# Retention in 64-token chunks for the first twelve rows too: 64x64 products, two of a row's four product lists one burst late

## The chip, the cores and the metric

The kernel runs on one core of a Trainium2 chip. Its metric is the device time of one execution in microseconds (us), lower is better. PE is the matrix engine TensorE, PEld its loading of weights, DVE is VectorE, ACT is ScalarE, POOL is GpSimd, and SP is the engine whose queue issues most DMAs. PSUM holds the sums of PE in eight banks of 512 f32 columns.

## The reference

Multi-head retention, and a feed-forward layer on its output. Shapes: 4 sequences, 8 heads, 768 tokens, 64 dimensions per head; the layer goes from 512 to 2048 and back, on 3072 tokens.

```python
gamma = 1.0 - 2.0 ** (-5.0 - np.arange(H))
scale = 1.0 / np.sqrt(D)
for t in range(S):
    state = gamma[None, :, None, None] * state + np.einsum('bhd,bhe->bhde', k[:, :, t], v[:, :, t])
    y[:, :, t] = scale * np.einsum('bhd,bhde->bhe', q[:, :, t], state)
x = y.transpose(0, 2, 1, 3).reshape(B * S, H * D)
h = x @ w_in
g = h * np.clip(h + 3.0, 0.0, 6.0) / 6.0
return g @ w_out
```

Over a piece of tokens the same y is the masked product of scores (q times k, only earlier tokens) with v, plus q times the state of the tokens before the piece, with the decay gamma laid on v and on y as powers.

## The kernel before, in words

**Rows.** The 3072 tokens are 24 rows of 128 tokens (six rows to a sequence), the eight heads are four pairs. `load(r)` fetches a row's four tiles: `kt` and `qt` (k and q with the dimension of a head pair on the 128 partitions), `vn` and `kn` (tokens on the partitions). The first eight rows (`AHEAD`) go into the large `early` tiles, with the odd rows' `kn` in buffers that later rows use (`SPARE`); the rows behind them use two buffers or one each (`BUFS`). Decays: rows 0 to 11 have them on v (`decay`: on ACT in eight instructions per row for rows 0 to 7, on GpSimd behind that) and on y (`load_decay` fetches the table `dq`); rows 12 to 23 have them on k and q (`scale`).

**Rows 0 to 11: `burst`.** PE's work for row r, and for the rest of row r-1, is one uninterrupted burst: products of the old row's q with its state (L268, eight, 64x64 weights, 128 columns); scores of the new row (L281, two per head, 64x64 weights, 128 and 64 columns) into `sc`, two PSUM banks; the old row's masked scores `am` with its v (L292, eight, 128x64 weights, 128 columns) into y; then DVE takes y times `dq` (L301) and `split` makes of it a high and a low part (ACT, DVE; L140, L141) as x. Last come the new row's sums of k times v (L314, eight, 128x64 weights) into `uz`, which ACT copies to SBUF as the state of row r+1 (L323), and DVE masks the new scores (L327: 1024 columns, all of `sc`). `am`, `sc` and `y` have one buffer each.

**Rows 12 to 23: `chunk_burst`.** A row is two chunks of 64 tokens, and all its products are 64x64 with 64 columns, in four lists of 16: `scores`, `sums` (into `uz`), `past` (q times state) and `inner` (masked scores times v). `together` sets two products of one list beside two of another. Half of `sc` and of `y` serves even rows and half odd rows; `keep(n)` is ACT's copy of `uz` as the state before chunk n. All its PE instructions are recorded as L349, its copies of `uz` as L353, and its mask product, 512 columns, as L392. `am` uses half of its tile; the other half is the buffer of the odd rows' `kn`.

**The layer.** `mm1(u, jj)` multiplies weight block jj with x of four rows (u): 12 matmuls of 128x512 into h (L464), three for each product of split numbers; ACT and DVE make g of it (L468, L469), which goes to memory. Three buffers of h. `build_w1` and `build_w2` make split f32 weights out of the 64-bit ones, on DVE and ACT (L122 to L141). Behind the last row (302 us) the output products run (L605).

**Order.** PE's order is written out by hand: bursts 0 to 4, then `mm1` for u = 0, with bursts 5 to 8 between its first four blocks; then blocks of u = 0 and u = 1 by turns, with bursts 8 to 12 (rows 8 to 11) among those of u = 1, then u = 2 and on with the chunked rows. Burst 8 is in two parts (old row, new row). `keep_busy` adds matmuls without use behind early bursts. The instructions of the other engines are ordered by a planner at compile time, by the order of the text and its own estimate of when each is ready; on the chip each engine keeps that order.

Of the kernel before, what the change touches and what calls it, by code (L numbers as in the profile page):

```python
# [28 lines left out]
def retention_ffn(ctx: ExitStack, tc: tile.TileContext, qkv, w_in, w_out, dvs, dqs, dkc, dqc, dmc, out, B, H, S, D):  # L29
# [37 lines left out]
    cst_sb = const.tile([P, ROWS_B, H], F32, name="cst_sb")  # L67
    nc.scalar.dma_start(out=cst_sb.rearrange("p n h -> p (n h)"), in_=dvs)
# [3 lines left out]
    mask = const.tile([P, 2, NPAIR // 2, P], F32, name="mask")  # L72
    nc.gpsimd.memset(mask, 1.0)
    for a in range(2):
        for b in range(2):
            m = mask[b * D : (b + 1) * D, a]
            nc.gpsimd.affine_select(
                out=m, in_=m, pattern=[[0, NPAIR // 2], [1, P]], compare_op=ALU.is_ge, fill=0.0, base=-D * (a ^ b), channel_multiplier=-1
            )
    ccst = const.tile([P, ROWS_B, 2 * NPAIR], F32, name="ccst")  # L80
# [112 lines left out]
    nc.vector.memset(sc, 0.0)  # L193
# [3 lines left out]
    def load(r):  # L197
# [7 lines left out]
        for i, (x, n) in enumerate((("kt", 1), ("qt", 0), ("vn", 3), ("kn", 2))):  # L205
            o = r % 2 * 4 + i
            if r < AHEAD and o < 7:
                t[x] = early[r // 2 * 2][:, o]
            elif x == "kn" and r > CHUNKED and r % 2:
                t[x] = both["am"][:, 1]  # L210
            else:
                tag = SPARE[r // 2] if r < AHEAD else f"l{x}"
                t[x] = apool.tile([P, NPAIR, P], F32, tag=tag, name=nm(x), bufs=BUFS[tag])
            m = NPAIR * P
            if x == "kn" and r % ROWS_B == ROWS_B - 1:
                m = m // 2 if r >= CHUNKED else 0
            if m:
                nc.sync.dma_start(out=t[x].rearrange("p h n -> p (h n)")[:, 0:m], in_=qkv[r, n][:, 0:m])
        if r >= CHUNKED:
            t["vn"], t["kn"] = (  # L220
                t[x].rearrange("p h n -> p (h n)").rearrange("p (c a e) -> p c a e", c=2, e=D) for x in ("vn", "kn")
            )
# [14 lines left out]
    def decay(r):  # L237
        v = rows[r]["vn"].rearrange("p a (h e) -> p (a h) e", h=2)
        if r < AHEAD:
            for h in range(H):  # L240
                nc.scalar.activation(  # L241
                    out=v[:, h], in_=v[:, h], func=AF.Copy, scale=cst_sb[:, r % ROWS_B, h : h + 1]
                )
        else:
            nc.gpsimd.tensor_tensor(
                out=v, in0=v, in1=cst_sb[:, r % ROWS_B, :, None].to_broadcast([P, H, D]), op=ALU.mult
# [12 lines left out]

    def burst(r, new=True, old=True):  # L260

        new, old = new and rows.get(r), old and rows.get(r - 1)
        if old:
            old["y"] = ps_a.tile([P, 2, NPAIR, P], F32, tag="y", name=nm("y"))
            if "state" in old:
                for p in range(NPAIR):
                    for h, pr in enumerate(halves):
                        nc.tensor.matmul(  # L268
                            place_y(old["y"], p, h),
                            old["state"][pr, p],  # L270
                            old["qt"][pr, p],
                            start=p < 2,
                            stop=False,
                            skip_group_check=True,
                        )
        if new:
            for p in range(NPAIR):
                for c in range(2):
                    for h, pr in enumerate(halves):
                        tokens = slice(0, P) if c == 0 else halves[1]  # L280
                        nc.tensor.matmul(  # L281
                            sc[halves[h ^ p % 2 ^ c], h, place_am(p, h), tokens],
                            new["kt"][pr, p, halves[c]],
                            new["qt"][pr, p, tokens],
                            start=True,
                            stop=True,
                            skip_group_check=True,
                        )
        if old:
            for p in range(NPAIR):  # L290
                for h in (p % 2, 1 - p % 2):
                    nc.tensor.matmul(  # L292
                        place_y(old["y"], p, h),
                        old["vn"][:, p, halves[h]],
                        old["am"][:, h, place_am(p, h)],
                        start=p < 2 and "state" not in old,
                        stop=True,
                        skip_group_check=True,
                    )
            x = apool.tile([P, NPAIR, P], F32, tag="xr", name=nm("xr"))  # L300
            nc.vector.tensor_tensor(  # L301
                out=x.rearrange("p (h a) n -> p h a n", h=2),
                in0=old["y"][:, :, 0 : NPAIR // 2],
                in1=old["dq"].rearrange("p (h a) n -> p h a n", h=2),
                op=ALU.mult,
            )
            split(*x_place(r - 1), x)
            del rows[r - 1]
        if new:
            n = r % ROWS_B  # L310
            if n < ROWS_B - 1:
                for p in range(NPAIR):
                    for pr in halves:
                        nc.tensor.matmul(  # L314
# [330 lines left out]
def chunked(rows):  # L645

    return rows // 2
# [87 lines left out]
```

## Time and profile before

| | |
|---|---|
| Time, three runs | 587.98, 589.79, 589.87 us; median 589.79 |
| Profiled execution | 588.39 us, span 586.7 us from the first to the last instruction |
| Granted PE clock, mean | 0.996 |
| First h (`mm1`) | starts at 30.3 us, and with more than one matmul at 31.8 |
| Bursts of rows 0 to 11 | 6 to 142 us |
| Chunked rows | 142 to 302.7 us |
| Output products | from 302.7 us on, L605 231.5 us of PE |

In the tables of groups, a line gives source line, engine, operation, output and inputs, shapes, count, busy time in all, mean ns of one, and idle time ahead of it with what ended it. In lists in order of time, the first number is the start in us, the second the time taken, and a bracket gives the idle time before and what released it. Matmuls are pipelined, and one's end is modelled, so the time of a run of them is taken from start to start.

### The profile page before, as it was taken

The page shows a single profiled execution, that of the slowest core. Times are in us where ns is not written, and L with a number is a line of the kernel's source. Part 1 is how long each engine was busy: PE and PEld are TensorE (multiplying, and loading weights), DVE is VectorE, ACT ScalarE, POOL GpSimd, SP SyncE. Part 2 cuts the span into 40 slices and gives each one's busy share as a digit, 9 for nine tenths or more (in the row PEclk, how much of TensorE's full clock was granted, in tenths as well). Part 3 has the DMA queues.
Part 4 walks back from the last instruction along what each step waited for, and adds up shares of the span by engine and source line. Part 5 has one row for each costly group of instructions (what it writes and reads, how often), then busy time and mean ns, then how long its engine had stood idle before and what let it go on. Part 6 is the DMA issues. An engine that isn't in the chain of part 4 may idle for free.

```text
span 586.7 us, 11328 instructions
## 1 busy us (share of the span) xinstructions
PE 571.7 (97%) x4604; PEld 469.8 (80%) x4604; DVE 416.2 (71%) x589; ACT 249.4 (43%) x393; POOL 36.5 (6%) x39
## 2 busy tenths in 40 slices
PE   8888999999999999999999999999999999999997
PEld 7776788787788888888888888888888888888885
DVE  4879999999533498333225989769786697866881
ACT  5674545444423344332324555434335344344430
POOL 1010000200211121122000000000000000000000
PEclk9989999999999999999999999999999999999999
DMA  8974777565865467565243557564844747635611
GB/s 319 391 280 162 238 246 258 205 228 199 278 207 191 168 226 256 179 184 175 92 131 121 180 206 242 171 223 142 271 161 144 226 142 276 218 95 193 214 73 72
DMA packets 59028, 117.05 MB, mean 200 GB/s; under 512 B 5984, under 2 KB 6624, under 8 KB 58976
## 3 DMA queue, kind: packets, MB, share of 16 engines
q1 hardware_dynamic: 44864, 91.01, 47.4%
q10 hardware_dynamic: 14112, 25.33, 11.4%
q8 instruction: 36, 0.59, 0.4%
q14 instruction: 16, 0.13, 0.1%
HBM read 84.85 MB, written 31.46 MB: 198 GB/s over the span
## 4 chain that ended last, share of the span: by engine, by line
PE 78%; DVE 14%; DMA 3%; issue 3%; ACT 1%; SPq 1%; ACTq 0%; DVEq 0%
PE o L605 39%; PE h L464 33%; DVE g L469 2%; DVE we L131 2%; PE uz L349 2%; DMA st<-in_w_in 2%; DVE wb L128 2%; DVE am L327 2%; PE sc L349 1%; DVE ww L134 1%; PE y L349 1%; DVE w L141 1%; DVE x L141 1%; DMA early<-in_qkv 1%; DVE xr L301 1%
## 5 line engine op out<-in xcount | busy, mean ns | idle before, releaser
L464 PE MATMUL h<-x,w 128*128 128x512 f32 x1152 | 271.1, 394 | 3.9 <-DVE g L469 1.8
L464 PEld LDWEIGHTS h<-x,w 128*128 128x128 f32 x1152 | 215.4, 189 | 52.2 <-DVE g L469 2.9
L605 PE MATMUL o<-gc,w 128*128 128x512 f32 x1008 | 231.5, 392 | 0.0
L605 PEld LDWEIGHTS o<-gc,w 128*128 128x128 f32 x1008 | 189.2, 188 | 42.1
L469 DVE SCALAR_TENSOR_TENSOR g<-g,h 128x512 f32<-128x512 f32 x96 | 65.3, 683 | 84.6 <-ACT g L468 84.6
L468 ACT ACTIVATE g<-h,three 128x512 f32<-128x512 f32 x96 | 65.3, 684 | 100.6 <-PE h L464 88.6
L140 ACT ACTIVATE gc<-gv 128x1024 fp32r<-128x1024 f32 x48 | 50.8, 1060 | 64.7 <-PE o L605 54.2
L141 DVE TENSOR_TENSOR gc<-gv,gc 128x1024 fp32r<-128x1024 f32 x48 | 58.6, 1221 | 23.8 <-ACT gc L140 23.8
L140 ACT ACTIVATE gc<-spare 128x1024 fp32r<-128x1024 f32 x36 | 38.2, 1061 | 50.3 <-PE o L605 39.9
L141 DVE TENSOR_TENSOR gc<-spare,gc 128x1024 fp32r<-128x1024 f32 x36 | 43.9, 1219 | 9.8 <-ACT gc L140 9.8
L140 ACT ACTIVATE w<-ww 128x384 fp32r<-128x384 f32 (+2 forms) x34 | 18.7, 555 | 48.6 <-DVE ww L134 46.1
L126 ACT ACTIVATE we<-we,ebias 128x512 int32<-128x512 int32 x32 | 22.9, 717 | 11.9 <-DVE we L122 11.9
L134 DVE SCALAR_TENSOR_TENSOR ww<-wb,we 128x512 f32<-128x512 f32 x32 | 25.3, 790 | 0.6
L235 POOL TENSOR_TENSOR qs<-qt,dq 128x512 f32<-128x512 f32 x12 | 16.8, 1397 | 96.7 <-PE y L349 74.1
L128 DVE SCALAR_TENSOR_TENSOR wb<-st,wb 128x512 f32<-128x512 uint32 x32 | 22.0, 686 | 0.3
L131 DVE SCALAR_TENSOR_TENSOR we<-st,we 128x512 int32<-128x512 int32 x32 | 22.1, 691 | 0.0
L141 DVE TENSOR_TENSOR w<-ww,w 128x384 fp32r<-128x384 f32 (+2 forms) x34 | 19.9, 590 | 3.1 <-ACT w L140 3.1
L96 DVE TENSOR_TENSOR spare<-gv 128x1024 f32<-128x1024 f32 x12 | 14.6, 1220 | 6.4 <-DMA gv<-gd 6.4
L122 DVE TENSOR_SCALAR we<-st 128x512 int32<-128x512 int32 x32 | 13.5, 421 | 7.7 <-DMA st<-in_w_in 7.4
L93 DVE TENSOR_TENSOR spare<-spare,gv 128x1024 f32<-128x1024 f32 x12 | 14.7, 1221 | 5.4 <-DMA gv<-gd 5.4
L241 ACT ACTIVATE early<-early,cst_sb 128x64 f32<-128x64 f32 x64 | 16.4, 336 | 4.3 <-DMA early<-in_qkv 4.3
L93 DVE TENSOR_TENSOR gv<-gv 128x1024 f32<-128x1024 f32 x12 | 14.7, 1223 | 4.8 <-DMA gv<-gd 4.5
(73 smaller groups left out, 392.7 us busy)
## 6 DMA issues: line engine op xcount, KB each, us to landing
gd<-g ACTq DMA_DIRECT2D x96, 256.0 KB, 2.6
gv<-gd SPq DMA_DIRECT2D x48, 512.0 KB, 4.9
gv<-gd SPq DMA_DIRECT2D x48, 256.0 KB, 3.1
st<-in_w_in SPq DMA_DIRECT2D x16, 512.0 KB, 4.1
st<-in_w_out SPq DMA_DIRECT2D x16, 512.0 KB, 3.7
early<-in_qkv SPq DMA_DIRECT2D x28, 256.0 KB, 6.0
kt<-in_qkv SPq DMA_DIRECT2D x16, 256.0 KB, 3.8
qt<-in_qkv SPq DMA_DIRECT2D x16, 256.0 KB, 4.6
```

Of the source, the lines that this page charges most:

```text
L93: return nc.vector.tensor_tensor(out=out_, in0=a, in1=b, op=ALU.subtract)
L126: nc.scalar.activation(out=e, in_=e, func=AF.Relu, scale=8.0, bias=ebias)
L128: nc.vector.scalar_tensor_tensor(out=y, in0=lo.bitcast(U32), scalar=2.0**-32, in1=b, op0=ALU.mult, op1=ALU.add)
L131: nc.vector.scalar_tensor_tensor(out=e, in0=hi, scalar=-2147483648, in1=e, op0=ALU.bitwise_and, op1=ALU.bitwise_or)
L134: nc.vector.scalar_tensor_tensor(out=w, in0=y, scalar=2.0**-20, in1=e.bitcast(F32), op0=ALU.mult, op1=ALU.mult)
L140: nc.scalar.activation(out=hi, in_=src, func=AF.Copy)
L141: nc.vector.tensor_tensor(out=lo, in0=src, in1=hi, op=ALU.subtract)
L349: nc.tensor.matmul(out_, lhs, rhs, start=start, stop=True, skip_group_check=True)
L464: nc.tensor.matmul(h, t[:, o, a], xs[u][b][:, k], start=k + n == 0, stop=(k, n) == (NK - 1, 2), skip_group_check=True)
L468: relu = nc.scalar.activation(out=g, in_=h, func=AF.Relu, bias=three)
L469: ins = nc.vector.scalar_tensor_tensor(out=g, in0=g, scalar=6.0, in1=h, op0=ALU.min, op1=ALU.mult)
L605: nc.tensor.matmul(acc[i][h] if last else acc[i][:, h], w2c[j][:, RIGHT[i], x, h], gc[:, y, jj], start=j == 0 and n == 0, stop=j == NFP - ...
```

## The change

Rows 0 to 11 take the products of the chunked rows, with their own decays. The layout of q, k, v is by chunk for all rows, and tables fall to match (`dvs` goes, `ccst` is loaded at the start in its place; its columns now scale v). The mask becomes 64x64 per head, repeated, and the mask product 512 columns wide (`weigh`, shared). `sc`, `y` and `am` are used by halves for all rows; `sc` is no longer cleared. `burst` issues, for the old row, the sums over chunk 0 beside the products with the state ahead of chunk 0, ACT's copy of `uz`, then the scores of the new row beside the old row's inner products, the mask product, then the old row's sums over chunk 1 beside the products with the state just copied, and another copy. So sums, states and inner products all belong to row r-1, scores to row r. The last row of a sequence loads the first half of its `kn`, which it did not need before.

```diff
-    cst_sb = const.tile([P, ROWS_B, H], F32, name="cst_sb")
-    nc.scalar.dma_start(out=cst_sb.rearrange("p n h -> p (n h)"), in_=dvs)
+    ccst = const.tile([P, ROWS_B, 2 * NPAIR], F32, name="ccst")
+    nc.scalar.dma_start(out=ccst.rearrange("p n h -> p (n h)"), in_=dkc)
...
-    mask = const.tile([P, 2, NPAIR // 2, P], F32, name="mask")
+    mask = const.tile([P, NPAIR, D], F32, name="mask")
...
-    nc.vector.memset(sc, 0.0)
...
-            elif x == "kn" and r > CHUNKED and r % 2:
+            elif x == "kn" and r > AHEAD and r % 2:
                 t[x] = both["am"][:, 1]
...
             if x == "kn" and r % ROWS_B == ROWS_B - 1:
-                m = m // 2 if r >= CHUNKED else 0
+                m = m // 2
...
+    def score(r):
+        new = rows[r]
+        s = chunks(sc, r)
+        new["am"] = chunks(both["am"], 0)
+        return [[(s[pr, c, p], new["kt"][pr, p, halves[c]], new["qt"][pr, p, halves[c]], True) for p, h, pr in sides] for c in range(2)]
+
+    def weigh(r, table):
+        nc.vector.tensor_tensor(
+            out=rows[r]["am"].rearrange("p c a t -> p c (a t)"),
+            in0=chunks(sc, r).rearrange("p c a t -> p c (a t)"),
+            in1=table[:, None, :].to_broadcast([P, 2, NPAIR * D]),
+            op=ALU.mult,
+        )
+
     def burst(r, new=True, old=True):
         new, old = new and rows.get(r), old and rows.get(r - 1)
+        scores = score(r) if new else [[], []]
+        sums, past, inner = ([[], []] for _ in range(3))
         if old:
+            y, n = both["y"][:, r % 2], (r - 1) % ROWS_B
+            for p, h, pr in sides:
+                for c in range(2):
+                    out_ = y[halves[1 - h], p, halves[c]]
+                    if c == 0 or n < ROWS_B - 1:
+                        sums[c].append((uz[pr, p], old["kn"][pr, c, p], old["vn"][pr, c, p], n + c + p == 0))
+                    if n + c:
+                        past[c].append((out_, ("state", c, pr, p), old["qt"][pr, p, halves[c]], c + p == 0))
+                    inner[c].append((out_, old["vn"][pr, c, p], old["am"][pr, c, p], n + c + p == 0))
+        together(sums[0], resolve(past[0], r - 1))
+        if sums[0]:
+            keep(2 * r - 1)
+        together(scores[0], inner[0])
+        together(scores[1], inner[1])
         if new:
+            weigh(r, mask.rearrange("p a n -> p (a n)"))
+        together(sums[1], resolve(past[1], r - 1))
+        if sums[1]:
+            keep(2 * r)
         if old:
             x = apool.tile([P, NPAIR, P], F32, tag="xr", name=nm("xr"))
+            nc.vector.tensor_tensor(out=x, in0=y, in1=old["dq"], op=ALU.mult)
             split(*x_place(r - 1), x)
             del rows[r - 1]
...
         decay(0)
+        both["am"] = apool.tile([P, 2, NPAIR, P], F32, tag="am", name=nm("am"), bufs=1)
+        both["y"] = ps_a.tile([P, 2, NPAIR, P], F32, tag="y", name=nm("y"))
...
             if r == AHEAD:
-                nc.sync.dma_start(out=ccst.rearrange("p n h -> p (n h)"), in_=dkc)
                 nc.sync.dma_start(out=cmask, in_=dmc)
```

All matmuls of the old `burst` fall away with this. `resolve` puts the state that is there by then in place of its name. `chunk_burst` takes its scores and mask product from `score` and `weigh`, with the work that it had.

More of the change, by code (lines that the diff above doesn't have):

```diff
@@ L263, in burst @@
         if old:
[L264 to L275, printed above, removed]
@@ L276, in burst @@
-        if new:
[L277 to L288, printed above, removed]
@@ L289, in burst @@
-        if old:
[L290 to L299, printed above, removed]
-            x = apool.tile([P, NPAIR, P], F32, tag="xr", name=nm("xr"))
[L301 to L306, printed above, removed]
+            y, n = both["y"][:, r % 2], (r - 1) % ROWS_B
@@ L307, in burst @@
             split(*x_place(r - 1), x)
             del rows[r - 1]
[L309 to L314, printed above, removed]
-                            uz[pr, p],
-                            new["kn"][:, p, pr],
-                            new["vn"][:, p, pr],
-                            start=n == 0 and p == 0,
-                            stop=True,
-                            skip_group_check=True,
-                        )
-                before[r + 1] = apool.tile([P, NPAIR, D], F32, tag="state", name=nm("state"), bufs=3)
-                nc.scalar.activation(out=before[r + 1], in_=uz, func=AF.Copy)
-            if r in before:
-                new["state"] = before.pop(r)
-            new["am"] = apool.tile([P, 2, NPAIR, P], F32, tag="am", name=nm("am"), bufs=1)
-            nc.vector.tensor_tensor(
-                out=new["am"].rearrange("p h a n -> p h (a n)"),
-                in0=sc.rearrange("p h a n -> p h (a n)"),
-                in1=mask.rearrange("p a b n -> p (a b n)")[:, None, :].to_broadcast([P, 2, NPAIR * P]),
-                op=ALU.mult,
-            )
@@ L334, in x_place, with resolve @@
+    def resolve(todo, r):
+        return [(out_, before[2 * r + lhs[1]][lhs[2], lhs[3]], rhs, start) for out_, lhs, rhs, start in todo]
     def x_place(r):
@@ L357, in chunk_burst @@
         new, old = rows.get(r), rows.get(r - 1) if r > CHUNKED else None
-        if r == CHUNKED:
-            both["y"] = ps_a.tile([P, 2, NPAIR, P], F32, tag="y", name=nm("y"))
-            both["am"] = apool.tile([P, 2, NPAIR, P], F32, tag="am", name=nm("am"), bufs=1)
-        sums, scores, past, inner = ([[], []] for _ in range(4))
-        sides = [(p, h, halves[h]) for p in range(NPAIR) for h in range(2)]
+        sums, past, inner = ([[], []] for _ in range(3))
+        scores = score(r) if new else [[], []]
         if new:
-            s = sc[:, r % 2].rearrange("p a n -> p (a n)").rearrange("p (c a n) -> p c a n", c=2, n=D)
-            new["am"] = both["am"][:, 0].rearrange("p a n -> p (a n)").rearrange("p (c a n) -> p c a n", c=2, n=D)
             for p, h, pr in sides:
-                for c in range(2):
-                    scores[c].append((s[pr, c, p], new["kt"][pr, p, halves[c]], new["qt"][pr, p, halves[c]], True))
                 first = r % ROWS_B == 0 and p == 0
@@ L391, in chunk_burst @@
         if new:
-            nc.vector.tensor_tensor(
-                out=new["am"].rearrange("p c a t -> p c (a t)"),
-                in0=s.rearrange("p c a t -> p c (a t)"),
-                in1=cmask[:, None, :].to_broadcast([P, 2, NPAIR * D]),
-                op=ALU.mult,
-            )
+            weigh(r, cmask)
         if old:
@@ L724 @@
         "in_w_out": lay_w_out(moe_w_out),
-        **{f"in_decays_{n}": a for n, a in zip("vykqs", constants(H, S, D))},
+        **{f"in_decays_{n}": a for n, a in zip("ykqs", constants(H, S, D))},
     }
```

60 lines of the change are left out of this document (21 added, 39 removed).

## The prediction

> **What bounds the kernel now.** I read the page's busy shares first, then busy times by stretch, then the chain that ended last in order of time, then the orders on TensorE (PE) and ScalarE (ACT) around the bursts of rows 0 to 11.
>
> ```profile
> PE 571.7 (97%) x4604; PEld 469.8 (80%) x4604; DVE 416.2 (71%) x589; ACT 249.4 (43%) x393; POOL 36.5 (6%) x39
> ```
>
> The whole is a PE kernel. But the change touches only what runs before 142 us, so the shares there count. Columns: stretch, its length, busy time of each engine (instructions), granted PE clock, DMA share, GB/s.
>
> ```profile
> core 0: us, PE busy (x) PEld busy (x) DVE busy (x) ACT busy (x) POOL busy (x), PEclk, DMA share, GB/s
> 17.60:31.80 14.20, 10.21 (x191) 8.51 (x188) 13.75 (x22) 10.55 (x33) 0.00 (x0) 1.00 1.05 391
> 31.80:41.00 9.20, 9.20 (x86) 7.36 (x87) 5.79 (x10) 6.06 (x21) 0.59 (x1) 0.81 0.88 313
> 41.00:60.00 19.00, 16.87 (x217) 13.15 (x217) 18.65 (x31) 9.58 (x19) 1.75 (x2) 1.00 0.47 162
> 60.00:94.00 34.00, 34.00 (x259) 27.86 (x257) 33.50 (x60) 16.74 (x29) 1.26 (x1) 1.00 0.72 242
> 94.00:134.60 40.60, 38.88 (x290) 31.36 (x288) 40.27 (x78) 18.20 (x32) 4.47 (x3) 1.00 0.64 213
> 160.00:300.00 140.00, 139.98 (x1765) 115.85 (x1764) 62.65 (x107) 47.77 (x84) 22.40 (x19) 1.00 0.55 184
> ```
>
> From 17.6 to 31.8 VectorE (DVE) is full (13.75 of 14.20) and PE is not; from 41 to 134.6 DVE stays full and PE has gaps that shrink; from 160 PE alone is full. The chain says the same (start, us, what):
>
> ```profile
> 19.77 1.13 DVE am L327
> ...
> 31.80 4.39 PE h L464 x11
> ...
> 127.38 0.74 DVE am L327
> ...
> 157.64 11.10 PE h L464 x48
> 170.78 11.13 PE h L464 x48
> ...
> 302.66 49.19 PE h L464 x216
> 351.85 231.33 PE o L605 x1008
> ```
>
> The masking of the scores, am on L327, stands on the chain nine times, the first and last of which are these. Behind 160 the time is a sum of matmuls that the change leaves alone, so the question is by how much it moves the point where PE leaves the last old burst.
>
> **What the change costs and saves, part by part.** (1) The mask product. Old rows mask 1024 columns, new rows 512, and the later rows already do the latter:
>
> ```profile
> L327 DVE TENSOR_TENSOR am<-sc,mask 128x1024 f32<-128x1024 f32 x12 | 14.6, 1214 | 0.0
> L392 DVE TENSOR_TENSOR am<-sc,cmask 128x512 f32<-128x512 f32 x12 | 8.3, 688 | 5.6 <-PE y L349 5.6
> ```
>
> 1214 - 688 = 526 ns for each of 12 rows, 6.3 us of DVE. Three (rows 2 to 4) lie between 17.6 and the first product h at 31.8, where DVE idles 0.45 us in all: 3 x 0.526 = 1.6 us earlier. Row 5's lies beside the h of 4.39 us and its ACT work, so I give it nothing; rows 6 to 11 give 6 x 0.526 = 3.2 us on DVE's path. DVE's path thus ends 4.8 us earlier.
>
> (2) PE's path. The old bursts, from their first instruction to the next h:
>
> ```profile
> 36.11 0.67 PE L268 MATMUL y<-early,state 64*64 64x128 f32 x16
> ...
> 38.40 3.03 PE L464 MATMUL h<-x,w 128*128 128x512 f32 x12
> ...
> 48.77 0.90 PE L281 MATMUL sc<-early 64*64 64x128 f32 x32 [1.63 <-DVE am L327]
> ...
> 51.09 3.06 PE L464 MATMUL h<-x,w 128*128 128x512 f32 x12
> 54.08 0.67 PE L268 MATMUL y<-early,state 64*64 64x128 f32 x16
> ...
> 55.70 3.38 PE L464 MATMUL h<-x,w 128*128 128x512 f32 x13
> 59.57 2.79 PE L464 MATMUL h<-x,w 128*128 128x512 f32 x11 [0.50 <-DVE x L141]
> 62.30 0.90 PE L281 MATMUL sc<-qt,kt 64*64 64x128 f32 x32
> 63.13 0.69 PE L314 MATMUL uz<-vn,kn 128*64 128x64 f32 x16
> 63.74 5.75 PE L464 MATMUL h<-x,w 128*128 128x512 f32 x24
> 69.42 0.67 PE L268 MATMUL y<-qt,state 64*64 64x128 f32 x16
> ...
> 72.18 22.06 PE L464 MATMUL h<-x,w 128*128 128x512 f32 x96
> ...
> 111.68 8.46 PE L464 MATMUL h<-x,w 128*128 128x512 f32 x36 [0.86 <-DVE g L469]
> ...
> 134.66 5.78 PE L464 MATMUL h<-x,w 128*128 128x512 f32 x24 [0.92 <-DVE g L469]
> ...
> 141.99 1.15 PE L349 MATMUL sc<-qt,kt 64*64 64x64 f32 x32
> 142.97 0.63 PE L349 MATMUL uz<-vn,kn 64*64 64x64 f32 x16
> ```
>
> A full burst takes 72.18 - 69.42 = 2.76 us (bursts 6, 9 and 10 are of this kind), one without the sum over keys 38.40 - 36.11 = 2.29 (5 and 11), one without a state 2.32 (7), the half with the old row alone 1.62 (8 and 12), with the new row alone 1.44 (8). Together 3 x 2.76 + 2 x 2.29 + 2.32 + 2 x 1.62 + 1.44 = 19.9 us.
>
> A chunked row's 64 products take the gap between two runs of h in the chain: 170.78 - (157.64 + 11.10) = 2.04 us, with its in-burst waits. The new burst issues the same four interleaved lists in another pairing: each still sets products of a head's own half beside products into the other half. Lists alone cost nearly as much: 16 scores by themselves took 142.97 - 141.99 = 0.98 us, 0.49 per list, where 2.04 / 4 = 0.51 is a pair's. So bursts 5, 9, 10 and 11 take 2.04, those with a list missing (6, 7, 8 and 12) 2.1, and row 8's scores alone 0.98: 4 x 2.04 + 4 x 2.1 + 0.98 = 17.5. PE work: -2.3 us.
>
> One row against that saving, records of 64x64 products:
>
> ```profile
> L349 PE MATMUL sc<-qt,kt 64*64 64x64 f32 x384 | 13.3, 219 | 0.0
> ```
>
> 384 for 12 rows of 16 products are two records each, so a row of 64 products is 128 records in 2.04 us, 16 ns each; I take that. [...]
>
> (3) The wait that the change adds. In a new burst PE sums chunk 0 into uz, ACT copies uz (keep), and only then may the sum over chunk 1 and the products with that state run, with PE's following h queued behind them. The old burst needed its state one burst later. How late ACT's copy stands behind the old uz:
>
> ```profile
> 43.55 0.64 PE L314 MATMUL uz<-early 128*64 128x64 f32 x16
> ```
>
> ```profile
> 46.78 0.36 ACT L323 ACTIVATE state<-uz 128x256 f32<-128x256 f32 x1
> ...
> 64.81 0.37 ACT L323 ACTIVATE state<-uz 128x256 f32<-128x256 f32 x1
> ...
> 73.60 0.36 ACT L323 ACTIVATE state<-uz 128x256 f32<-128x256 f32 x1
> ```
>
> The uz above ended at 44.19 and its copy began 2.6 us later; the one at 63.13 ended at 63.82, copy 1.0 later; the one that ended by 72.2 (ahead of the h of 72.18), 1.4 later. ACT keeps its order, and sat there before weight copies for which DVE was late (us in total before 310 us, times, longest):
>
> ```profile
> ACT w L140 <- DVE ww L134: 35.2, 17, 3.6
> ```
>
> The two lists of scores and inner products, 1.02 us, cover the copy's own 0.37 and 0.65 of lag. Upper end: lag as here, mean 1.7, so 1.0 us for each of the eight bursts 5 to 12, 8 us (nearer 12 if all were like the first). Lower end: 0, since the copy is ready some 2 us earlier in the burst and may get an earlier place in ACT's order; in the chunked rows, where ACT is a third busy, the 2.04 us holds it already. Below 0 is excluded: it adds a wait and removes none. I take the middle, 4 us.
>
> (4) Waits that go. PE's gaps of 1.63, 0.50, 0.86 and 0.92 us (the bracketed rows above), 3.9 us in all, are PE ahead of DVE. The first also falls to the doubled score buffer; the others are taken up by the stalls of (3), in which DVE catches up. Late next is then the g of DVE, which ends 4.8 us earlier by (1).
>
> (5) At nothing. ACT's second copy per row, some 10 x 0.37 us, lies in its free half; where ACT is full, its price is in (3). The constants swap one load of 24 KB for another on ACT's queue and drop one from SP's; the cleared score buffer leaves an idle DVE at the start. Row 5's keys, 128 KB more on a DMA that moves 391 GB/s, put rows 6 and 7 and a weight block 0.33 us back; cover: their first use is behind the h of 31.8. If that cover is gone, 0.33. That key tile holds one of the two buffers of qt until burst 6, so qt of row 8 is issued some 7 us later on SP, with the row's v, k and row 9's v perhaps queued behind and GpSimd's decay of v behind them; they are wanted at 62 us, 20 us on. Keys of rows 9 and 11 move to the free half of am: no wait. The elementwise x on DVE and the decay of v on ACT and GpSimd keep their sizes. Row 11's added half of keys is loaded under cover of 50 us of h.
>
> **Sum.** PE's path: -1.6 (first h) - 2.3 (bursts) + 4 (stalls) - 3.9 (gaps) = -3.8 us. DVE's path: -4.8. The later one counts: -3.8. The profiled execution took 588.39 us for a span of 586.7; 588.4 - 3.8 = 584.6. The three runs have their mean, 589.2, 0.8 above it and their median, 589.79, 1.4 above; I put a median of the new kernel 0.8 above: 585.4.
>
> **Rivals.** A, the load bound: the DMA share is 1.05 until 31.8, so rows and weights may come no earlier, and with row 5's keys 0.33 later. Against: DVE is full in that stretch. Then +0.3 instead of -1.6, in all -1.9, 587.3. Either side of the bound of 0.3%, which is 1.8 us.
>
> B, on the other side: the wait for the state copy. Place: the middle of bursts 5 to 12, PE behind ACT behind DVE's weight building. For it speaks the lag of 2.6 us, against it that DVE gets shorter and PE's lead with it. At 12 us of stalls instead of 4, the sum is +4.2, 593.4. It makes the kernel no faster from 7.8 us, 1.0 a burst.
>
> C, the clock. After the PE gaps around 30 us a stretch ran at half clock:
>
> ```profile
> 33.00:34.00 1.00, 1.00 (x4) 0.50 0.95 369
> ```
>
> The 11 h there took 4.39 us, 0.40 each, against 22.06 / 96 = 0.23 at 72 us: 1.8 us lost. New bursts 1 to 4 give PE some 0.7 us less work each, in a stretch where it is already idle 4 of 14 us. Two more such stretches would cost 2 x 1.8 = 3.6 us: -0.2, 589.0. Against: before 31 us the clock stayed full with these gaps. [...]
>
> D, the best case: no stall at all, -7.8, 581.4. It is the lower end of my forecast.
>
> **Chances.** Forecast (D with it) 0.62, A 0.12, B 0.14, C 0.12. 0.3% is 1.8 us, about what this kernel's three runs can tell from nothing. Faster: 0.62 and half of A, 0.68. Same: C and half of A, 0.18. Slower: B, 0.14. The range for 8 in 10 runs from 581 (D) to 590 (A and C inside, B's far half out); the likeliest case's own is 581 to 588.
>
> **What would show it.** The am of rows 0 to 11 at 0.69 us; the first full-speed h near 30.2 instead of 31.8; bursts 9 to 11 as gaps near 2.0 us in PE's order of h, and the row 12 burst about 0.5 longer than before. A stall shows as PE idle in front of the second uz list with the copy of uz on ACT just before its end. PE should reach the unchanged rows (157.64 above) near 153.8. I am wrong if the copy of uz on ACT stands behind weight copies in most bursts, if the first h does not move, or if half clock shows before it.

## The result, and the profile after

The changed kernel is slower: 591.94 us in the median of eight runs (591.01 to 593.94), beside 588.93 for eight runs of the kernel before (587.98 to 589.87). The ratio is 1.0055, with a 95% interval of 1.0038 to 1.0071. The profiled execution took 592.13 us for a span of 590.4, 3.7 us more than before on both counts. The forecast, 585.4 in a range of 581 to 590, was wrong in sign.

The busy shares of the changed kernel, from its page, say that PE has 1.8 us less work than before, DVE 6.9 less and ACT, at 43%, 4.4 more.

```profile
PE 569.9 (97%) x5180; PEld 470.7 (80%) x5180; DVE 409.3 (69%) x588; ACT 253.8 (43%) x405; POOL 33.9 (6%) x37
```

So the time is in waits. The waits of PE in the changed kernel (engine, what waited, what it waited for: us in total, times, longest):

```profile
PE uz L326 <- ACT state L330: 6.0, 4, 2.2
PE idle L369 <- issue: 2.3, 1, 2.3
PE h L422 <- DVE g L427: 1.9, 1, 1.9
PE y L326 <- ACT state L330: 1.8, 1, 1.8
...
PE h L422 <- ACT x L138: 1.2, 1, 1.2
PE y L326 <- DVE xr L303: 0.9, 1, 0.9
PE h L422 <- DVE x L139: 0.6, 1, 0.6
```

Five of them, 7.8 us together, are for ACT's copy of `uz`. The largest single wait, 2.3 us, is of another kind: PE stands in the middle of its filler matmuls (L369) ahead of the first h, and "issue" means that the profile shows nothing that it waited for. Where all of them lie, PE in order of time (start, us, instruction, idle before in brackets):

```profile
13.93 0.27 PE L326 MATMUL uz<-early 64*64 64x64 f32 x2 [2.07 <-ACT state L330]
16.80 0.37 PE L326 MATMUL uz<-early,kn 64*64 64x64 f32 x2 [2.17 <-ACT state L330]
...
33.84 0.38 PE L369 MATMUL idle<-mask 128*128 128x128 f32 x2 [2.34 <-issue]
33.98 3.02 PE L422 MATMUL h<-x,w 128*128 128x512 f32 x12
...
45.55 0.68 PE L326 MATMUL y<-early,state 64*64 64x64 f32 x16 [1.84 <-ACT state L330]
...
62.20 0.50 PE L422 MATMUL h<-x,w 128*128 128x512 f32 x1 [1.18 <-ACT x L138]
63.34 4.38 PE L422 MATMUL h<-x,w 128*128 128x512 f32 x11 [0.64 <-DVE x L139]
...
101.08 0.27 PE L326 MATMUL uz<-vn,am 64*64 64x64 f32 x2 [1.03 <-ACT state L330]
...
126.05 0.27 PE L326 MATMUL uz<-vn,kn 64*64 64x64 f32 x2 [0.74 <-ACT state L330]
...
162.26 2.11 PE L422 MATMUL h<-x,w 128*128 128x512 f32 x8
```

Two of the five are in the bursts ahead of the first h, for which the prediction had no such wait; three are in bursts 6, 10 and 11. The first h starts later (33.98 where the row before had 31.80) but at full clock (1.00 granted from 33.98 to 36.90), 3.02 us for its 12 instead of 4.38 for 11, so it ends 0.8 later. The half clock of the kernel before is not what its bursts always meet: all nine kernels below that have the old bursts in front ran these 11 products in 2.76 to 2.81 us. Against them the first h would end some 2.4 us late (36.92 - (36.11 - 1.6)). And the first h on the x of rows 4 to 7 waits at 61 us, and 11 of its products then take 4.38 instead of 2.79. The stretches by granted clock of the changed kernel show three slow places (PEclk, the third number from the end); the kernel before has 1.00 in each of these stretches, and its slow stretch was the one at 33 us.

```profile
12.00:18.00 6.00, 1.90 (x76) 1.76 (x80) 2.21 (x4) 4.20 (x15) 0.00 (x0) 0.80 1.05 392
18.00:24.00 6.00, 5.50 (x167) 4.98 (x161) 5.80 (x11) 4.86 (x16) 0.00 (x0) 0.63 1.05 391
46.00:52.00 6.00, 6.00 (x94) 4.73 (x94) 5.97 (x11) 2.98 (x6) 0.00 (x0) 0.72 0.81 275
60.00:66.00 6.00, 4.18 (x12) 2.86 (x11) 6.00 (x12) 3.60 (x7) 0.00 (x0) 0.78 0.70 242
```

Against the row of before at the same work, PE is +0.8 us late at the end of the first h block (36.92 against 36.11), +1.6 behind burst 7, +5.35 when row 8's scores begin (67.65 against 62.30), +4.3 behind burst 9, +4.7 behind row 13 (162.26 against 157.57), +3.7 at the end. The whole loss is there by 68 us. Behind it the shorter bursts nearly cancel with the stalls of bursts 10 and 11 and the wait of 1.88 us for g at 138 us.

### The profile page after: what moved, and what is told of

The parts are those of the page before. It is cut to its first block, busy times and chain, and to the rows that moved or that the text cites. A ratio compares the mean times of both kernels' runs of the same rounds, so it can differ in the third digit from the quotient of the medians.

```text
span 590.4 us, 12497 instructions
## 1 busy us (share of the span) xinstructions
PE 569.9 (97%) x5180; PEld 470.7 (80%) x5180; DVE 409.3 (69%) x588; ACT 253.8 (43%) x405; POOL 33.9 (6%) x37
## 4 chain that ended last, share of the span: by engine, by line
PE 74%; DVE 1%; DMA 0%; issue 0%; ACT 0%; DVEq 0%; ACTq 0%
PE o L563 39%; PE h L422 31%; PE uz L326 2%; PE sc L326 1%; PE y L326 1%; DVE g L427 0%; DMA dq<-in_decays_y 0%; DVE ws L91 0%; DVE we L129 0%; DVE w L139 0%; DVE kept_v L507 0%; ACT state L330 0%; DVE wb L121 0%; DVE we L120 0%; DVEq L673 0%
## 5 line engine op out<-in xcount | busy, mean ns | idle before, releaser
L139 DVE TENSOR_TENSOR gc<-gv,gc 128x1024 fp32r<-128x1024 f32 x48 | 58.6, 1221 | 18.9 <-ACT gc L138 18.9
L139 DVE TENSOR_TENSOR gc<-spare,gc 128x1024 fp32r<-128x1024 f32 x36 | 43.9, 1220 | 8.2 <-ACT gc L138 8.2
L132 DVE SCALAR_TENSOR_TENSOR ww<-wb,we 128x512 f32<-128x512 f32 x32 | 24.1, 754 | 0.5
L129 DVE SCALAR_TENSOR_TENSOR we<-st,we 128x512 int32<-128x512 int32 x32 | 22.7, 711 | 0.0
L139 DVE TENSOR_TENSOR w<-ww,w 128x384 fp32r<-128x384 f32 (+2 forms) x34 | 20.0, 592 | 3.5 <-ACT w L138 3.3
L330 ACT ACTIVATE state<-uz 128x256 f32<-128x256 f32 x44 | 16.5, 376 | 11.1 <-PE y L326 9.5
L237 ACT ACTIVATE early<-early,ccst 128x64 f32<-128x64 f32 x64 | 17.1, 337 | 6.8 <-DMA early<-in_qkv 6.7
```

The costliest lines, as they stand in the source:

```text
L129: nc.vector.scalar_tensor_tensor(out=e, in0=hi, scalar=-2147483648, in1=e, op0=ALU.bitwise_and, op1=ALU.bitwise_or)
L132: nc.vector.scalar_tensor_tensor(out=w, in0=y, scalar=2.0**-20, in1=e.bitcast(F32), op0=ALU.mult, op1=ALU.mult)
L139: nc.vector.tensor_tensor(out=lo, in0=src, in1=hi, op=ALU.subtract)
```

## The experiments

Times are medians; "before" is the kernel before, run beside them on the same chip: 588.88 for the first four, 588.15 for the next four, 588.87, 588.71 and 588.42 for the last three groups.

**Without the second copy.** e1 takes the changed kernel's copy in the middle of a burst away; the products with the state of chunk 1 read the older state, so part of the result leaves chunk 0 out.

```diff
         together(sums[0], resolve(past[0], r - 1))
-        if sums[0]:
-            keep(2 * r - 1)
```

> The changed kernel without the copy of uz in the middle of a burst; the products with the state ahead of a row's second chunk use the state ahead of its first one (and fall away in the first row of a sequence), so that state is left out of the computation. Theory W (PE waits inside the burst for ScalarE's copy, which stands behind decays and weight copies in ScalarE's strict order): the gaps of 2.07, 2.17, 1.84, 1.03 and 0.74 us go, the slow clock that follows them goes, the first full-speed h starts near 31 us, time 584 to 587 us. Rival P (the 64x64 products in this pairing, or the planner's other order, cost the time, and the wait only fills room that was idle anyway): within 1.5 us of the changed kernel's 591.9.

591.88, ratio 1.0056 [1.0033, 1.0079]: the same as with the copy. The stalls in bursts 6, 10 and 11 are gone, but other waits stand in their place: 4.4 us for a state copy in front, 4.6 us in five waits for g and 2.5 for x. The wait in front ends at 16.25 us, where the two waits of the changed kernel end at 16.80, so it isn't the added copy that sets that time. The theory that the copy alone costs the time falls.

**The chunked rows' order.** e2 gives rows 0 to 11 the pairing of `chunk_burst`: the sum of chunk 0 in the row's own burst, so that each copy has a burst or half a burst more.

```diff
+        if new:
+            for p, h, pr in sides:
+                sums[1].append((uz[pr, p], new["kn"][pr, 0, p], new["vn"][pr, 0, p], r % ROWS_B + p == 0))
...
-        together(scores[0], inner[0])
-        together(scores[1], inner[1])
+        together(scores[0], past[1])
+        together(scores[1], inner[0])
+        together(sums[1], inner[1])
```

> The changed kernel with the pairing of the later rows for rows 0 to 11: sums over chunk 0 in the row's own burst at its end, sums over chunk 1 at the start of the next, so both states of a row exist before its products need them; two copies of uz a row as before, and only the last list of a burst waits for one. Theory W: y no longer waits for a copy of the same burst and the wait stands at the burst's end beside the inner products; a part of the stalls goes, 588 to 590 us. Rival L (ScalarE's load: two copies a row between decays make x late whatever the order): 591 to 593 us.

593.63, 1.0091 [1.0070, 1.0112]. The first h comes at 35.2 instead of 34.0, the waits for copies come to 5.5 us in five. More slack for each copy did not help: three of them, 1.0, 1.5 and 1.6, are still ahead of the first h. Two waits without a releaser, 2.4 and 2.2 us, stand there too.

**Filler.** e3 puts `keep_busy(8)` ahead of the last lists of bursts 1 to 4, against the half clock at 16 to 20 us (0.50 granted in the changed kernel).

```diff
+        keep_busy(8 if 1 <= r <= 4 else 0)
         together(sums[1], resolve(past[1], r - 1))
```

> The changed kernel with 8 idle matmuls of 128x128 (about 2.2 us) ahead of the last lists of bursts 1 to 4, where PE waits for the copy, so that PE is busy there. Theory C (the waits cost mainly through the half clock that follows them before the first h): no slow clock between 12 and 24 us, bursts 2 and 3 at full speed, 1.5 to 2.5 us less, 589.5 to 590.5. Theory W alone: the bursts are faster but wait as long for ScalarE, 591 to 593.

595.83, 1.0124 [1.0083, 1.0165]. The clock rose to 1.00 at 12 to 18 us, where it had been 0.80, and to 0.93 at 18 to 24, where it had been 0.63, but the first full run of h came at 39.35, 5.4 us later. Two waits without a releaser, 4.0 us together (2.8 in the changed kernel), are part of that. So the filler cost more than it gave, and what the half clock there costs by itself isn't shown.

**Rows 0 to 5 as before.** e4 keeps the old bursts, layout and masks for the first sequence and has the new ones for rows 6 to 11.

```diff
+    NEAR = ROWS_B
...
+            if r == NEAR:
+                burst(r, new=False)        # burst: that of the kernel before
...
+                near_burst(r, old=False)   # near_burst: that of the changed kernel
```

> Rows 0 to 5 by the old burst, rows 6 to 11 by the new one. Theory F (the loss is made in the front, where ScalarE has the decays, and rows 6 to 11 gain on PE): first full-speed h near 31.8 us, 586 to 588.5 us. Theory W (each burst that waits loses, the late ones too): the stalls of bursts 10 and 11 stay, 588.5 to 590 us.

590.48, 1.0023 [1.0005, 1.0041]. The first h is back where it was (30.46 and 31.94, its 11 at full clock in 2.80), so the new bursts in front are what moved it. At 117.8 us PE was 2.25 us ahead of the kernel before; then it lost that in one wait of 2.76 in burst 11. ACT in that wait, in order of time:

```profile
118.53 0.52 ACT L149 ACTIVATE w<-ww 128x384 fp32r<-128x384 f32 x1 [1.59 <-DVE ww L143]
120.06 0.63 ACT L149 ACTIVATE w<-ws 128x512 fp32r<-128x512 f32 x1 [1.00 <-DVE ws L102]
...
121.78 0.37 ACT L425 ACTIVATE state<-uz 128x256 f32<-128x256 f32 x1
```

PE waits for that copy from 119.45 on, and it stands in ACT's order behind two copies of an output-weight (w2) build, which wait for DVE. That weight is first used by the output products, behind 300 us.

**The order on DVE around x of row 7.** In the changed kernel DVE finishes that x at 63.3, in the one before at 59.5 (x, row 7, L141 in the first; L139 in the second):

```profile
58.83 0.69 DVE L141 TENSOR_TENSOR x<-xr,x 128x512 fp32r<-128x512 f32 x1
```

```profile
62.61 0.68 DVE L139 TENSOR_TENSOR x<-xr,x 128x512 fp32r<-128x512 f32 x1
```

From 36 us up to that x, DVE has done five of the steps `we` of a weight build (L129) where it had done three (L131): the compile-time list has more builds ahead of it. e5 queues builds 7 to 9 behind that x, in the changed kernel; e6 does the opposite to the kernel before, and queues row 7's product with its decay on DVE behind build 7, which is called one block earlier for it.

```diff
# e5
+            with tc.issue_after(done_x[7]):   # builds 7 to 9
                 build_w1(n_w1)
# e6, in before.py
+            with tc.issue_after(built[7]):    # row 7
                 nc.vector.tensor_tensor(out=x, in0=y, in1=dq, op=ALU.mult)
```

> The changed kernel with one edge more for the planner: VectorE's work for weight blocks 7 to 9 is queued behind x of row 7. In the changed kernel VectorE had built blocks 4 to 7 and most of 8 ahead of x of row 7; before, 4, 5 and most of 6. Theory O (the planner, which orders VectorE at compile time, puts some 1.7 more block builds ahead of x of rows 4 to 7; PE then waits for x near 61 us and its clock halves behind that wait): x of row 7 done near 59 instead of 63.3 us, the gaps of 1.18 and 0.64 us and the slow stretch of h of 4.38 us go, 3 to 4 us less than 591.9, 588 to 589. Theory W (only the wait inside bursts): no change, 591 to 593.

> The kernel before with the opposite edge: weight block 7 is built ahead of x of row 7 (y times decay of row 7 is queued on VectorE behind block 7). Nothing else of the change. Theory O: x of row 7 comes 3 us later, PE waits for it near 59 us and runs h at half clock behind it, 2 to 4.5 us more than before, 591 to 593.5. If order is not what costs: within 1 us of before.

e6: 593.18, 1.009 [1.0075, 1.0105]; the order alone costs the kernel before 5.0 us. PE in e6:

```profile
63.91 0.79 PE L468 MATMUL h<-x,w 128*128 128x512 f32 x1 [4.76 <-ACT x L140]
65.05 4.12 PE L468 MATMUL h<-x,w 128*128 128x512 f32 x10 [0.35 <-DVE x L141]
```

e5: 593.25, 1.0098 [1.0066, 1.0130]: no gain. Yet the x wait is gone, h runs through at full clock, and burst 9 starts 4.3 us earlier than in the changed kernel (70.10 against 74.41). PE and its waits in e5:

```profile
57.68 5.74 PE L423 MATMUL h<-x,w 128*128 128x512 f32 x24
64.43 5.74 PE L423 MATMUL h<-x,w 128*128 128x512 f32 x24
```

```profile
PE uz L327 <- ACT state L331: 8.6, 6, 2.6
PE y L327 <- ACT state L331: 3.9, 2, 2.6
```

The waits for state copies in bursts 10, 11 and 12 took 1.7, 2.6 and 2.6 us back, and PE leaves burst 12 at 149.07, to the hundredth where the changed kernel leaves it.

**Last lists one h block later.** e7 (on e4, bursts 9 to 12) and e8 (on the changed kernel, bursts 5 to 7 too) put an h block between the middle copy and the lists that need it.

```diff
+        if r in LATER:
+            tails.append(rest)   # last lists, copy, x: issued behind the next mm1
```

> Rows 0 to 5 by the old burst as in the run before of that kind (590.5 us), rows 6 to 11 by the new one, and in bursts 9 to 12 the last lists (sums over chunk 1, products with the state just copied, and what follows) come one block of h later, in burst 12 behind the next row's scores. ScalarE's copy then has 2.8 us of h as cover. Theory W for the late rows: the stalls of 2.76 and 0.89 us in bursts 11 and 12 go, 3 to 4 us less, 586.5 to 587.5, below the kernel before. If the copy is later still, or g waits in its place: 589 to 591.

> The changed kernel with the last lists of bursts 5, 6, 7, 9, 10 and 11 one block of h later, in burst 12 behind the next row's scores. The bursts of the front stay. Theory W: the stalls of 1.84, 1.03 and 0.74 us and the slow clock behind the first go, 4 to 5 us less, 587 to 588. Theory O: x of rows 4 to 6 comes no earlier, the wait near 61 us and its slow clock stay, 589 to 591.

e7: 588.96, 1.001 [0.9997, 1.0023], even with before; the stalls of bursts 10 and 11 are gone and two waits for g, 1.4 us in all, came. The waits for the copy in burst 12 (0.8) and for x at 59 us (2.2) stood in e4 too. e8: 594.69, 1.0127 [1.0107, 1.0148]; in front of 60 us the later x is what PE needs next (4.7 us for xr, 6.8 for copies).

**Are DVE's weight builds what PE waits for?** DVE was over 99% busy in both kernels from 103 to 138 us, and seven w2 builds lie in the stretch up to 150. e9 to e12 moved the calls of three of them later in the text (in the changed kernel, before, e7, e5).

```diff
-    WHEN = {1: (9, 12, 15), 2: (4, 8, 12), 3: (4, 12), 4: (4, 12), 5: (4, 6, 8, 10, 12, 14)}
+    WHEN = {2: (4, 8, 12), 3: (4, 8, 12), 4: (4, 8, 12), 5: (3, 4, 6, 8, 10, 12, 14)}
```

> The changed kernel with the three output weight builds that ran among the blocks of u = 1 moved to u = 3, 4 and 5, where VectorE is half idle. Theory D (until some 146 us VectorE's fixed list, weight builds included, sets the pace, and a new burst, unlike an old one, must wait for ScalarE's place in that list): the stalls of bursts 10 to 12 (1.03, 0.74 us) and the wait for g of 1.88 us go, 3 to 4.5 us less, 587.5 to 589. The wait for x near 61 us and the late first h stay. If only the front costs: 591 to 593.

> The kernel before with the same three builds moved: the control. Theory D: its two waits for g, 0.86 and 0.92 us, go, 1.5 to 2.5 us less than before, 586.5 to 587.5. If these builds do not set PE's pace: within 1 us of before.

> Rows 0 to 5 by the old burst, 6 to 11 by the new one with its last lists one block of h later in bursts 9 to 12, and the three builds moved. Without the move this took 589.0 us, no better than before, though PE's bursts are shorter. Theory D: what the bursts save on PE now counts, since VectorE no longer sets the pace: 2 to 3 us below the control, 584 to 585.5. Rival: the shorter bursts are worth nothing here even so: as the control.

> The changed kernel with weight blocks 7 to 9 queued behind x of row 7, and the three builds moved. The first alone took away the wait for x near 61 us (4.3 us at that point) but lost it again to stalls of 1.7, 2.6 and 2.6 us in bursts 10 to 12. Theory D: with less ahead of the copies these stalls do not come back, so both gains add: 583.5 to 586. If the stalls are ScalarE's own order and not VectorE's load: 588 to 593.

591.97, 588.34, 588.90, 592.62 (ratios 1.0052, 0.9991, 1.0006, 1.0059): nothing moved, and the traces say why: the builds still ran at 103 to 148 us. The planner took the builds forward although their calls stood later. So these runs tell nothing of the theory. e13 to e16 hold the builds with an edge, in the same four kernels:

```diff
+            with tc.issue_after(last_g):   # DVE's g of u = 1, jj = NF - 1
                 build_w2(n_w2)
```

> The changed kernel with the output-weight (w2) builds held by a real edge behind VectorE's last g of x tile 1 (near 146 us), so the planner can't pull any of the seven of them into the stretch before. Theory D (VectorE's list, filled with builds that are not yet due, sets TensorE's pace from 60 to 146 us): about 33 us of VectorE work leaves that stretch, the waits of bursts 10 and 11 for the state copy (1.0, 0.7) and for g at 138 us (1.9) go; the x of row 7 still comes near 63 us, so 588 to 589.5. Rival S (the waits come from ScalarE's own order and the chain of burst, copy, burst, not from VectorE's builds): the waits stay within 0.5 us and the time stays at 591.5 to 592.5. Rival M (the builds held back cost as much later, after 150 us, by waits for w2): 592 or more, with new waits for g or w after 150 us.

> The kernel before with the same hold of the w2 builds: the control. Theory D: its waits for g (0.9 and 0.9) and for x of row 7 (0.5) are all that VectorE's list costs it, so 586.5 to 588, that is 1 to 2 us faster. Rival S: 588.5 to 589.5, no change. Rival M: 589.5 or more.

> The kernel with the old bursts for rows 0 to 5, the new ones for rows 6 to 11, and the last list of bursts 9 to 12 one block of h later, with the same hold. It was even with the kernel before, because waits for g (1.4), the state copy (0.8) and x (2.2) took what its shorter bursts gave. Theory D: these go, 584 to 586. Rival S: they stay, 588.5 to 589.5. Rival M: 590 or more.

> The changed kernel with builds 7 to 9 of the input weights queued behind the x of row 7 on VectorE, and the same hold. By itself that order gained 4.3 us at burst 9 and lost it in waits for the state copy in bursts 10 to 12 (1.7, 2.6, 2.6). Theory D: those waits go with the w2 builds and the gain stays: 585.5 to 588. Rival S: they stay at 5 us or more together: 591.5 to 593. Rival M: 593 or more.

All four were slower than the kernel before: 596.38, 593.07, 593.52 and 594.46 (ratios 1.0134, 1.0083, 1.0075, 1.0096). But look at the stretch the hold was for. The columns from the second are length, then busy us of PE, PEld, DVE, ACT, POOL; the changed kernel, then e13, then e14:

```profile
103.00:138.00 35.00, 34.24 (x268) 27.78 (x266) 34.76 (x76) 17.64 (x32) 3.50 (x3) 1.00 0.68 233
```

```profile
103.00:138.00 35.00, 35.00 (x274) 29.01 (x273) 10.38 (x16) 9.67 (x15) 3.34 (x3) 1.00 0.46 162
```

```profile
103.00:138.00 35.00, 35.00 (x229) 28.61 (x229) 10.53 (x16) 8.90 (x13) 3.38 (x3) 1.00 0.41 144
```

DVE falls from 34.8 to 10.4, PE has no wait left, and the h behind row 13 starts earlier in both kernels. That h on PE, in order of time, in before, e14 (before with the hold), e13 (changed with the hold) and e16 (e5 with the hold):

```profile
157.57 6.64 PE L464 MATMUL h<-x,w 128*128 128x512 f32 x28
```

```profile
153.22 5.05 PE L464 MATMUL h<-x,w 128*128 128x512 f32 x21
```

```profile
157.72 6.66 PE L422 MATMUL h<-x,w 128*128 128x512 f32 x28
```

```profile
155.65 2.58 PE L423 MATMUL h<-x,w 128*128 128x512 f32 x10
```

At this row e14 is 4.35 us ahead of the kernel before, and e13 4.54 (162.26 - 157.72) ahead of the changed one. Of e14's lead 0.94 is there at burst 9 already (68.48 against 69.42), ahead of every w2 build, so the hold brings about 3.4 us to the kernel before and 4.6 to the changed one, whose burst 9 stands where it stood (74.47 against 74.41). The builds do cost PE that time, in both; the changed kernel stays 4.5 us behind, 6.0 lost ahead of burst 9 and 1.5 won behind it. Then all of it is paid back: the builds held run together behind 146 us, and e14's chunked rows wait, where before had no wait at these places:

```profile
168.93 0.27 PE L349 MATMUL uz<-vn,kn 64*64 64x64 f32 x2 [2.98 <-issue]
...
185.31 0.37 PE L349 MATMUL uz<-vn,am 64*64 64x64 f32 x2 [3.02 <-issue]
```

The profile names no releaser, and e17's expectation took the transfers of the rows for it. But these products add to `uz`, which ACT must have copied first, and each starts 0.1 us behind the end of that copy. ACT in e14, where the copies stand behind steps of the builds that wait for DVE:

```profile
167.26 0.72 ACT L126 ACTIVATE we<-we,ebias 128x512 int32<-128x512 int32 x1 [0.79 <-DVE we L122]
...
168.46 0.37 ACT L353 ACTIVATE state<-uz 128x256 f32<-128x256 f32 x1
...
183.84 0.52 ACT L140 ACTIVATE w<-ww 128x384 fp32r<-128x384 f32 x1 [3.02 <-DVE ww L134]
...
184.84 0.38 ACT L353 ACTIVATE state<-uz 128x256 f32<-128x256 f32 x1
```

e13, e15 and e16 have the same wait of 3.0 us near 172 us, it too ending 0.1 us behind a copy. It is the wait of e4 again, moved to where the builds now run.

The last two deal ten builds out over x tiles 2 to 4, each held behind the g before it: e17 in the kernel before, e18 in e7 with e5's order.

```diff
+    WHEN = {2: (3, 7, 11), 3: (3, 7, 11, 15), 4: (3, 7, 11), 5: (4, 6, 8, 10, 12, 14)}
+            with tc.issue_after(end):      # g of the block before
                 build_w2(n_w2)
```

> The kernel before with the ten output-weight (w2) builds of x tiles 1 to 4 dealt out over x tiles 2 to 4, each held behind VectorE's g of the h block before its new place, so that they neither fill VectorE before 146 us nor pile up just after it. Theory D (VectorE's list sets the pace from 60 to 146 us; the run that held all of them to 146 us left the row-12 burst 4.3 us earlier than the kernel before and lost it in two waits of 3.0 at 166 and 182 us for transfers behind the pile): the 4.3 us stay, 584 to 585.5. Rival S (what is gained there is lost again in waits further on whatever the builds' places): 588 or more, with waits of 3 us in bursts after 160 us.

> Old bursts for rows 0 to 5, new ones for rows 6 to 11, the last list of bursts 9 to 12 one h block later, builds 7 to 9 of the input weights queued behind the x of row 7 on VectorE, and the w2 builds dealt out as in the kernel before's run beside it. Theory D: the waits for x of row 7 (1.4 and 0.8, with 1.5 us at half clock) go too, so what is left of the change is the shorter bursts 9 to 12: 583 to 585, that is 0 to 1.5 us below its neighbour. Rival C (a ready list does not help the new bursts, which wait for the copies on ScalarE): 586 to 588, slower than its neighbour, with waits for the state copy of over 1 us in bursts 10 to 12.

592.88 and 592.69 (1.0081 [1.0068, 1.0093] and 1.0072 [1.0056, 1.0088]). Up to the output products all went as meant: PE has no wait from 63 us on, is 4.2 us ahead of before at the first output product in e17 (347.5 against 351.7), and e18 is ahead of e17 by 1.0 at row 13 (152.59 against 153.62) and 0.9 at 243 us. Then, PE in e17:

```profile
358.77 0.79 PE L606 MATMUL o<-gc,w 128*128 128x512 f32 x1 [5.52 <-ACT gc L140]
360.09 1.22 PE L606 MATMUL o<-gc,w 128*128 128x512 f32 x2 [0.52 <-DVE gc L141]
```

Before finished its last w2 build at 346.7, e17 at 354.5. The last two g are sent to memory at 350.3 and 351.5 instead of 351.9 and 353.3. But the load of g that PE then lacks, the fourth of this stage, is issued at 350.3 and lands at 357.6; in the kernel before the fourth was issued at 347.3. Why it comes later was not tried. The clock is 0.81 from 347 to 361 and 0.87 from there to 380, where before has 1.00. Waits of 6.0 us and the slow clock behind them take the 4.2 us and some 5 more. No version beats the kernel before; e7 and e11, and the kernel before with moved calls (e10), are even with it.

## Why the prediction was wrong, point by point

| us, up to row 13 | forecast | measured |
|---|---|---|
| first h (measured at its end) | -1.6 | +0.8 |
| bursts 5 to 12, stalls left out | -2.3 | -1.4 |
| stalls for the state copy in them | +4 | +3.6 |
| PE's other gaps behind 36 us | -3.9 | -0.2 |
| half clock behind 36 us | 0 | +3.1 |
| burst 13 | 0 | -0.9 |
| sum | -3.8 | +5.0 (4.7 by the rows) |

The bursts: a full one took 76.44 - 74.41 = 2.03 us (forecast 2.04), the others 2.0 to 2.3, burst 8's halves 2.36 and 1.08, and row 12's cost 0.4 more as said. am takes 0.69 us, as forecast. The bursts thus save 1.4 us, 0.9 less than forecast, most of it in bursts 5, 10 and 11 at 2.2 instead of 2.04 and in burst 8. The stalls in bursts 5 to 12, 1.84 + 1.03 + 0.74, come to the forecast sum by some luck: the prediction spread 4 us over eight bursts, and three of them hold it all. These steps held in the main.

**First failed step: the first h (1).** It was worked out from DVE alone (three am of 0.526). Two other things held it: ACT's order, and a stop of PE that no other engine explains. ACT in the changed kernel, bursts 1 and 2, and then DVE:

```profile
12.56 1.05 ACT L237 ACTIVATE early<-early,ccst 128x64 f32<-128x64 f32 x4
13.52 0.36 ACT L330 ACTIVATE state<-uz 128x256 f32<-128x256 f32 x1
15.65 0.83 ACT L237 ACTIVATE early<-early,ccst 128x64 f32<-128x64 f32 x3 [1.78 <-DMA early<-in_qkv]
16.38 0.36 ACT L330 ACTIVATE state<-uz 128x256 f32<-128x256 f32 x1
...
17.12 0.62 ACT L138 ACTIVATE x<-xr 128x512 fp32r<-128x512 f32 x1
```

```profile
17.77 0.69 DVE L139 TENSOR_TENSOR x<-xr,x 128x512 fp32r<-128x512 f32 x1 [2.37 <-ACT x L138]
```

The first copy stands behind a weight copy and four decays, and PE waits for it 2.07 us. The second stands behind decays of a row whose transfer is late; PE waits for it 2.17 us, and so does the x behind it, for which DVE idles 2.37 us. DVE begins its next weight step at 18.38 us, where it began at 17.68, and the last x that the first h needs is done at 33.08 instead of 31.74, narrower masks and all. That is 1.3 of the 2.2 us by which the first h starts late. The other 0.9 are the filler wait of 2.34 us: PE takes up h at 33.98, where before it took it up 0.06 us behind that x. The prediction counted eight bursts, 5 to 12, for its wait and gave the four ahead of the first h none; its words on ACT's second copy ("where ACT is full, its price is in (3)") left them out. The stop it did not have at all; likely it is the load of instructions, of which the new bursts have more for PE (last section). Rival A had the load of the rows as a bound, at +0.3; it acts through ACT's decays. e4 shows that the front is the new bursts' doing; how much of it each of the two is worth at the end was not tried.

**Second failed step: waits that go (4).** The four named waits went, 3.9 us. New ones of 1.18, 0.64 and 1.88 stand in their place, 3.7. "Late next is then the g of DVE, which ends 4.8 us earlier" took DVE's saved time as slack. It is not: the list puts more builds into it, ahead of row 7's x. DVE was as full as before up to 138 us. e6 shows that this order alone can cost 5 us and e5 that undoing it gives 4.3 back; that the narrower mask is what made the planner change the order was not tried by itself.

**Third: the clock.** Rival C was given for the stretch ahead of 31 us. There the clock did halve (0.50 granted from 16 to 22 us), and e3 doesn't settle what that cost. What is counted is behind it: 1.5 us behind burst 6 (12 h in 4.53 instead of 3.02, clock 0.50 at 47 to 49 us) and 1.6 at 63 us (clock 0.50 at 64 to 66), each just behind a wait. The prediction had nothing for half clock behind 36 us. Rival B's place was right: in bursts 6, 10 and 11 ACT's copy stands behind weight steps, the first of which waits 1.7, 1.5 and 1.9 us for DVE. Its size (12 us) was not; its time, 593.4, was the nearest of all by luck, as its 12 us of stalls were 3.6.

What stays open: how much of the loss ahead of burst 9 (5.0 us in the changed kernel, 6.0 between e13 and e14) each part holds. e16 puts 2.1 us (157.72 - 155.65) on the order of builds 7 to 9, and e18, with the builds dealt out, another 3.1 on the old bursts of rows 0 to 5 and the later last lists together. With all of these, the shorter bursts of rows 6 to 11 are worth 1.0 us at row 13 and nothing at the end.

## What to carry to other kernels

Where engines run strict orders made at compile time, time saved on a full engine is no slack: find what the list will put into it, and whose result then stands behind. A wait added in the middle of a burst is priced by the engine that answers it, in every stretch where that engine is late, the first one above all. And a gain in mid-kernel counts only if the stage behind is ready earlier too: here 4.2 us carried over 200 us of matmuls fell to one late load and the slow clock behind it (0.81 and 0.87 granted), at the last boundary. Last, an idle time to which the profile gives no releaser should be held against what the program itself requires: two such waits here were for a state copy, and another was likely for instructions.

## What the runs showed of the hardware

Two DVE steps beside GpSimd products took twice their time, 1.41 and 1.53 us where 0.69 is their size. GpSimd in the changed kernel, then DVE:

```profile
40.32 1.04 POOL L239 TENSOR_TENSOR vn<-vn,ccst 128x512 f32<-128x512 f32 x1 [38.21 <-DMA vn<-in_qkv]
41.60 1.21 POOL L239 TENSOR_TENSOR vn<-vn,ccst 128x512 f32<-128x512 f32 x1 [0.24 <-DMA vn<-in_qkv]
```

```profile
40.49 1.41 DVE L126 SCALAR_TENSOR_TENSOR wb<-st,wb 128x512 f32<-128x512 uint32 x1
41.83 1.53 DVE L129 SCALAR_TENSOR_TENSOR we<-st,we 128x512 int32<-128x512 int32 x1
...
46.48 0.69 DVE L126 SCALAR_TENSOR_TENSOR wb<-st,wb 128x512 f32<-128x512 uint32 x1
```

Both ended some 0.55 us behind the end of a product beside them (41.90 behind 41.36, 43.36 behind 42.81). The profile does not show why. The 1.6 us fell on DVE ahead of row 7's x. In the kernel before, two steps beside the same two products took 0.4 us more there (0.82 and 0.94 for steps of 0.69; they too ended 0.55 behind a product), so 1.2 are new. Not each step beside a product was longer: there g (L469) took its 0.69 from 43.32 on, all of it beside the product of 43.01 to 44.31. The prediction let the decay on GpSimd keep its size, which it did (1.04 and 1.21), and did not ask about the DVE steps beside it.

Half clock followed a PE wait of 1.84 us (ended at 45.55; granted 0.50 from 47 to 49), but not one of 1.88 (138 to 139.9, granted clock 1.00 from 139 to 146): in these rows the length of a wait alone does not tell it. Nor did it come in every profile behind the same old bursts: the same 11 products took 4.38 us in the kernel before's (granted 0.50 from 33 to 34) and 2.80 in e4's, with waits of 0.62 and 0.98 us ahead of them in both.

PE stopped at places where the profile shows nothing that it waited for, and the stops lie behind landings of the instruction queue. In the ten traces with the new bursts in front there are 22 such stops of over 0.15 us ahead of 41 us, up to 3.2 us long, and each ends 1.2 to 1.6 us behind the landing of a packet of 16 KB of that queue: at 21.92 and 32.40 in the changed kernel, where PE goes on at 23.31 and 33.84. The ten traces with the old bursts in front have none. PE starts 1210 matmuls and weight loads ahead of 34 us in the changed kernel and 871 in the one before, and the DMA engines are full there (share 1.02 to 1.05 from 6 us on). No run changes the number of instructions alone, so that this is the cause is likely and not shown.
